# Loading token tile 2 in two partition halves on two queues, and turning it behind three K-blocks of v(0)

## The chip, the core and the metric

The kernel runs on one core of a Trainium2 chip. Its engines are TensorE (PE for matmuls, PEld for the loading of their weights), VectorE (DVE), ScalarE (ACT), GpSimd (POOL) and SyncE (SP, which here only issues DMAs). The metric is the device time of one execution in microseconds (us); a profiled execution has a span, from the first to the last instruction of the program, and a time of its own that is a little longer than the span.

## What is computed

The input x holds 2048 tokens of width 512 in bf16. Two branches read the same layer-normalised x, and both are added to x:

```python
xn = layernorm(x)                        # no scale, no shift
# branch A: linear attention, 32 heads of width 16
q, k, v = split(xn @ wqkv)               # wqkv is 512 x 1536
phi(z) = [softmax(z @ w_phi), softmax(-z @ w_phi)]
o = phi(q) @ (phi(k)^T v) / (phi(q) @ sum(phi(k)) + 1e-6)
# branch B: a gated product, inner width 1792
h = (xn @ w_gate) * (xn @ w_up)
out = x + o @ wo + h @ w_down
```

## The kernel before

**Tiles.** The tokens are cut into 16 tiles of 128 (tile t holds every fourth token of a block of 512). A tile of x is 128 partitions by 512 elements, 128 KB. Every product needs the normalised tile turned, so that the 512 features lie on partitions: four blocks of 128 features (the K-blocks 0 to 3), called `xnT` with the halves `("xnT", t, 0)` (K-blocks 0 and 1) and `("xnT", t, 1)` (K-blocks 2 and 3).

**The first four tiles.** Tiles 0 to 3 take a path of their own at the start of the program, because nothing else is there for TensorE to do. For such a tile the mean is taken in two halves of the row, one by ACT and one by DVE (`ln_mean_split`: the ACT instruction at L228 and the DVE instruction at L427, each followed by a short read of its accumulator). The mean is then subtracted by DVE (`ln_center_split` at L434 in two instructions for tiles 0 and 1, `ln_center_whole` at L439 in one for tiles 2 and 3). The scale by the standard deviation is deferred to later places. TensorE turns the centred tile by four 128x128 transposes (`x_transpose`, two calls of two transposes, L474), and ACT copies K-blocks 0 and 1 from PSUM to `xnT` (L228) while DVE copies K-blocks 2 and 3 (L483); for tile 1, DVE copies both halves.

**v of tiles 0 and 1.** `v_matmul(t, b, qs)` is a product of tile t with K-blocks of the v weights into PSUM bank b: one 128x512 matmul for each K-block (L247). The weights of K-block q are loaded by `load_v(eng, q)`, 128 KB each. K-blocks 0 and 1 of both tiles come first, then K-block 3 of both, then the four transposes of tile 2, then K-block 2 of both. Then come the four matmuls of v(2), the four transposes of tile 3, and the gate and up products, whose weights are `load_gu(..., 0, ...)`.

**What sets the order.** The loads of the start are a list written out by hand, each on SP's queue or on ACT's:

```python
    load_x(0, 1)
    load_x(1, 1, ACT)
    load_v(SP, 0)
    load_v(ACT, 1)
    load_x(2, 1)
    load_v(ACT, 3)
    load_v(SP, 2)
    load_x(3, 1)
    load_gu(SP, 0, (1,))
```

The compute steps of the start are pinned (`sc.pin`): every engine takes them in the order in which they are written. Later steps are placed by a planner (`_order`) with modelled costs. Each engine runs its own list strictly in order, and a step waits for the semaphores of the steps that it reads from. A step that reads data of two DMAs waits for two semaphores. The PE list, from the first real work on: transposes of tiles 0 and 1, K-blocks 0 and 1 of v(0) and v(1), and so on as above. In front of it stand eight `warm` matmuls on constants (L1001), the last of which waits for tile 0 of x.

Of the kernel before, what the change touches and what calls it, by code (L numbers as in the profile page):

```python
# [13 lines left out]
PE, ACT, DVE, POOL, SP = "PE", "ACT", "DVE", "POOL", "SP"  # L14
# [95 lines left out]
def bass_parallel_sum__linear_kernel_hedgehog__glu_gated_bilinear__prompt_kernel(  # L110
    nc: bass.Bass,
    A_x: bass.AP,
    A_wqkv: bass.AP,
    A_w_phi: bass.AP,
    A_wo: bass.AP,
    B_x: bass.AP,
    B_w_gate: bass.AP,
    B_w_up: bass.AP,
    B_w_down: bass.AP,
    out: bass.AP,  # L120
):
    with ExitStack() as es:
        _build(nc, es, A_x, A_wqkv, A_w_phi, A_wo, B_w_gate, B_w_up, B_w_down, out)


def _build(nc, es, A_x, A_wqkv, A_w_phi, A_wo, B_w_gate, B_w_up, B_w_down, out):
# [77 lines left out]
    def sb(name, lo, n):  # L204
        off = layout[name] + lo
        return arena[:, off:off + n]
# [4 lines left out]
    def sbf(name, lo, n):  # L211
        off = layout[name] + 2 * lo
        return arena[:, off:off + 2 * n].bitcast(F32)

    def bank(b, lo=0, n=512):
        return psum[:, b * 512 + lo:b * 512 + lo + n]

    def bank16(b, lo, n):
        return psum16[:, b * 1024 + lo:b * 1024 + lo + n]

    sc = _Sched()

    def act(out_ap, in_ap, reads, writes, func=ACTF.Copy, scale=1.0, bias=None, accum=None):
        kw = {} if bias is None else {"bias": bias}
        if accum is not None:
            kw["accum_out"] = accum
        n = out_ap.free_size()
        return sc.step(ACT, lambda e: e.activation(out=out_ap, in_=in_ap, func=func, scale=scale, **kw),  # L228
                       reads, writes, 130.0 + 0.833 * n)

    def dve(fn, reads, writes, n, rate=1.04):
        return sc.step(DVE, fn, reads, writes, 140.0 + rate * n)
# [7 lines left out]
    def mm(out_ap, pairs, reads, b, start=True, stop=True, skip=False, also=()):  # L240
        npair = len(pairs)

        def fn(e):
            ins = None
            for i, (l, r) in enumerate(pairs):
                kw = {"skip_group_check": True} if skip else {}
                ins = e.matmul(out_ap, lhsT=l, rhs=r, start=start and i == 0, stop=stop and i == npair - 1, **kw)  # L247
            return ins
        return sc.step(PE, fn, reads, [("ps", b), *also], npair * pe_cost(out_ap.free_size()))

    x_flat = A_x.flatten_outer_dims()
# [6 lines left out]
    def x_tile(t):  # L258
        return sb("x", t * 512, 512)

    def xnT(q, lo, n):
        return sb("xnT", q * S_TOK + lo, n)


    def rows(ap, t0, n):
        g, r = divmod(t0, 4)
        return ap[g * 512:(g + 1) * 512, :].rearrange("(p r) d -> p r d", r=4)[:, r:r + n, :]

    def load_x(t0, n, eng=SP):
        o = sb("x", t0 * 512, n * 512).rearrange("p (t d) -> p t d", t=n)  # L270
        i = rows(x_flat, t0, n)
        sc.dma(eng, lambda e: e.dma_start(o, i), [], [("x", t) for t in range(t0, t0 + n)], n * 131072)

    def xr_tile(t):
        return sb("xr", (t % 4) * 512, 512)

# [29 lines left out]
    def load_v(eng, q):  # L306
        load_w(eng, wv_v[:, q, :], A_wqkv[q * 128:(q + 1) * 128, 1024:1536], ("wv", q), 131072)
# [16 lines left out]
    load_x(1, 1, ACT)  # L324
    load_v(SP, 0)
    load_v(ACT, 1)
    load_x(2, 1)
    load_v(ACT, 3)
    load_v(SP, 2)
    load_x(3, 1)  # L330
# [63 lines left out]
    def xn_tile(t):  # L394
        return sb("xn", (t % 4) * 512, 512)

    mu = sbf("mu", 0, ND)
# [24 lines left out]
    mua = sbf("mua", 0, ND)  # L422

    def ln_mean_split(t):
        act(xn_tile(t)[:, 256:], x_tile(t)[:, 256:], [("x", t)], [("mu", t)], scale=1.0 / 512.0,
            accum=mu[:, t:t + 1])
        dve(lambda e: e.tensor_scalar(out=xn_tile(t)[:, :256], in0=x_tile(t)[:, :256], scalar1=1.0 / 512.0,  # L427
                                      scalar2=0.0, op0=ALU.mult, op1=ALU.add, accum_out=mua[:, t:t + 1]),
            [("x", t)], [("mua", t)], 256)

    def ln_center_split(t):
        for h in range(2):
# [5 lines left out]
    def ln_center_whole(t):  # L438
        dve(lambda e: e.tensor_scalar(out=xn_tile(t), in0=x_tile(t), scalar1=mua[:, t:t + 1],  # L439
                                      scalar2=mu[:, t:t + 1], op0=ALU.subtract, op1=ALU.subtract),  # L440
            [("x", t), ("mua", t), ("mu", t)], [("xn", t, 0)], 512, 0.27)
# [24 lines left out]
    def x_transpose(t, b, h, eng=ACT):  # L466
        n = NQ // 2
        qs = slice(h * n, (h + 1) * n)

        def fn(e):  # L470
            ins = None
            for i in range(n):
                q = h * n + i
                ins = e.transpose(bank16(b, i * 128, 128), xn_tile(t)[:, q * 128:(q + 1) * 128], ident)  # L474
            return ins
        sc.step(PE, fn, [("xn", t, h if t < 2 else 0), "ident"], [("ps", b)], n * 60.0)
        o = sb("xnT", 0, NQ * S_TOK).rearrange("p (q s) -> p q s", q=NQ)[:, qs, t * 128:(t + 1) * 128]
        i = bank16(b, 0, n * 128).rearrange("p (q s) -> p q s", q=n)
        w = [("xnT", t, h)]
        if eng == ACT:  # L480
            act(o, i, [("ps", b)], w)
        else:
            dve(lambda e: e.tensor_copy(out=o, in_=i), [("ps", b)], w, n * 128)  # L483
# [45 lines left out]
    def v_matmul(t, b, qs=((0, 1), (2, 3)), start=True, stop=True):  # L529
        for n, part in enumerate(qs):  # L530
            mm(bank(b), [(xnT(q, t * 128, 128), wv_v[:, q, :]) for q in part],
               ([("xnT", t, part[0] // 2)] if t < ND else [("xnT", t)]) + [("wv", q) for q in part], b,
               start=start and n == 0, stop=stop and n == len(qs) - 1)
# [398 lines left out]
    def out_pair(p, fill):  # L932
# [14 lines left out]
        def sum_w(k):  # L947
            return tw[k], two[k], [("tw", k), ("two", k)]
        x0 = xr_tile(t0)
        product((p, 1), BA, raw_a(t0, 0), raw_w(0, 0), True)  # L950
        seed(BB, BA)
# [6 lines left out]
        s7_2 = s7[:, None, :].to_broadcast([128, 2, 256])  # L958
        pool(lambda e: e.tensor_tensor(out=xs.rearrange("p (b c) -> p b c", b=2), in0=s7_2,  # L959
                                       in1=xr_tile(t1).rearrange("p (b c) -> p b c", b=2), op=ALU.add),  # L960
             ["s7", ("xr", t1 % 4)], ["xs"], 512)
        product((p, 3), BB, sum_a(2), sum_w(2))
# [34 lines left out]
    def warm(n, w=512, after=()):  # L997
        def fn(e):
            ins = None
            for _ in range(n):  # L1000
                ins = e.matmul(bank(7, 0, w), lhsT=nc.const_aps.tensor(1.0, (128, 128), BF16),  # L1001
                               rhs=nc.const_aps.tensor(1.0, (128, w), BF16), start=True, stop=True)
            return ins
        sc.step(PE, fn, after, [("ps", 7)], n * w * 0.8)

    warm(7)
    warm(1, 512, [("x", 0)])
    sc.pin = True
    ln_mean_split(0)
    ln_mean_split(1)  # L1010
    ln_center_split(0)
    ln_center_split(1)
    x_transpose(0, 2, 0)
    x_transpose(0, 3, 1)
    warm(1, 128)
    x_transpose(1, 4, 0, DVE)
    ln_mean_split(2)
    x_transpose(1, 5, 1, DVE)
    warm(1, 128)
    ln_center_whole(2)  # L1020
    for t in range(2):
        v_matmul(t, t, ((0, 1),), stop=False)
    for t in range(2):
        v_matmul(t, t, ((3,),), start=False, stop=False)
    x_transpose(2, 6, 0)
    x_transpose(2, 4, 1, DVE)
    for t in range(2):
        v_matmul(t, t, ((2,),), start=False)
    ln_mean_split(3)
    ln_center_whole(3)  # L1030
    (g0a, u0a, g0b, u0b), gate0 = up_unit(*ups.pop(0), pairs, 2)
# [363 lines left out]
```

## Time and profile before

| | |
|---|---|
| runs | 213.91, 214.06, 214.47, 214.66, 214.69 us (median 214.47) |
| profiled execution | 214.02 us, span 212.3 us |
| PE busy | 208.5 us, 98% of the span, 1476 matmuls |
| PEld busy | 125.2 us, 59% |
| DVE busy | 167.3 us, 79% |
| ACT busy | 143.7 us, 68% |
| POOL busy | 110.0 us, 52% |
| granted TensorE clock | 1.0 |
| DMA | 22.29 MB, mean 105 GB/s |

The busy time of an engine is the union of its instructions. Matmuls are pipelined: each appears in the trace with its own latency, so that consecutive ones overlap, and a short wait between two of them can lie under the tail of the first and not show as idle time. The distance from one start to the next tells more. A DMA appears twice: as the instruction on SP or ACT that issues it, and as its landing, some microseconds later, which is when its semaphore lets the readers go.

### The profile page before, as it was taken

How to read it: one execution, taken by the hardware profiler on the slowest of the kernel's cores; microseconds unless marked ns; L12 is line 12 of the kernel's file. 1: busy time of each engine (PE TensorE's matmuls, PEld its weight loads, DVE VectorE, ACT ScalarE, POOL GpSimd, SP SyncE). 2: the span in 40 equal slices, each digit the busy share in tenths (PEclk: the TensorE clock that was granted, in tenths of full speed). 3: DMA queues.
4: the chain of work that ended last, by engine and by line, in shares of the span. 5: the costliest groups of instructions: out<-in, count | busy, mean ns of one | idle time of the engine just before them, and what ended most of it. 6: DMA issues, size and time to landing. Idle time of an engine off the chain costs nothing.

```text
span 212.3 us, 4049 instructions
## 1 busy us (share of the span) xinstructions
PE 208.5 (98%) x1476; PEld 125.2 (59%) x1476; DVE 167.3 (79%) x281; ACT 143.7 (68%) x350; POOL 110.0 (52%) x137
## 2 busy tenths in 40 slices
PE   7999999999999999999999999999999999999995
PEld 2574444444544444444444444556888898899884
DVE  3777999986995647578699988986888898898622
ACT  4489899975789999988778977564534444432220
POOL 4031554540320366999995872004558659558540
PEclk9999999999999999999999999999999999999999
DMA  5999890799100140322720330414265746637411
GB/s 175 301 295 376 127 217 0 73 362 186 25 3 0 8 90 3 53 58 43 78 56 18 76 75 0 130 43 51 50 77 125 176 76 150 144 83 175 123 49 49
DMA packets 49251, 22.29 MB, mean 105 GB/s; under 512 B 38096, under 2 KB 47696, under 8 KB 49232
## 3 DMA queue, kind: packets, MB, share of 16 engines
q1 hardware_dynamic: 48272, 21.39, 46.0%
q10 hardware_dynamic: 960, 0.66, 1.0%
q8 instruction: 11, 0.18, 0.4%
q14 instruction: 8, 0.07, 0.2%
HBM read 11.03 MB, written 2.10 MB: 62 GB/s over the span
## 4 chain that ended last, share of the span: by engine, by line
PE 97%; DMA 1%; DVE 1%; issue 0%
PE ps L247 91%; PE ps L553 2%; PE ps L611 2%; DMA arena<-in_A_x_dram 1%; PE ps L381 1%; PE ps L474 1%; DVE arena L427 0%; DVE arena L924 0%; DVE arena L434 0%; PE ps L1001 0%
## 5 line engine op out<-in xcount | busy, mean ns | idle before, releaser
L247 PE MATMUL ps<-arena 128*128 128x512 bf16 (+2 forms) x1160 | 199.8, 330 | 0.0
L247 PEld LDWEIGHTS ps<-arena 128*128 128x128 bf16 (+1 forms) x1160 | 110.8, 98 | 73.1 <-ACT arena L228 0.9
L228 ACT ACTIVATE arena<-ps 128x512 bf16<-128x512 f32 (+3 forms) x117 | 58.6, 539 | 12.7 <-PE ps L247 8.0
L228 ACT ACTIVATE arena<-arena 128x32 f32<-128x32 f32 (+9 forms) x131 | 52.9, 423 | 11.0 <-DVE arena L506 6.8
L894 DVE TENSOR_TENSOR arena<-ps,arena 128x512 f16<-128x512 f32 (+1 forms) x56 | 38.3, 684 | 11.7 <-PE ps L247 6.1
L516 POOL TENSOR_TENSOR arena<-arena 128x1024 bf16<-128x1024 bf16 x16 | 31.8, 1995 | 26.4 <-ACT arena L228 26.4
L506 DVE TENSOR_REDUCE arena<-arena 128x64 f32<-128x1024 bf16 x32 | 38.2, 1211 | 7.8 <-ACT arena L228 7.6
L228 ACT ACTIVATE arena<-ps,arena 128x512 bf16<-128x512 f32 (+1 forms) x55 | 35.9, 671 | 10.9 <-PE ps L247 10.4
L855 POOL TENSOR_TENSOR arena<-arena 128x256 f16<-128x256 f16 x32 | 23.9, 756 | 14.1 <-DMA arena<-arena 12.9
L833 DVE TENSOR_TENSOR arena<-arena 128x896 f16<-128x896 f16 x32 | 26.0, 812 | 3.4 <-PE ps L247 3.4
L228 ACT ACTIVATE ps<-ps 128x256 f32<-128x256 f32 x24 | 8.8, 368 | 29.0 <-PE ps L247 27.0
L924 DVE SCALAR_TENSOR_TENSOR arena<-ps,arena 128x256 bf16<-128x256 f32 (+1 forms) x24 | 13.2, 566 | 8.8 <-PE ps L247 8.7
L773 POOL TENSOR_TENSOR arena<-arena 128x512 f16<-128x512 bf16 x14 | 16.3, 1174 | 5.7 <-DVE arena L894 5.2
L959 POOL TENSOR_TENSOR arena<-arena 128x512 f32<-128x512 f32 x8 | 9.5, 1191 | 17.0 <-ACT arena L228 17.0
L522 POOL TENSOR_TENSOR arena<-arena 128x512 bf16<-128x512 bf16 x16 | 16.9, 1059 | 0.8
L621 DVE TENSOR_TENSOR arena<-ps,arena 128x512 f16<-128x512 f32 x16 | 11.0, 686 | 1.3 <-ACT arena L228 0.5
L405 DVE BATCH_NORM_STATS2 arena<-arena 128x6 f32<-128x512 bf16 x16 | 10.4, 670 | 0.5 <-DMA arena<-in_A_x_dram 0.5
L520 POOL TENSOR_TENSOR arena<-arena 128x32 f32<-128x32 f32 x16 | 5.2, 326 | 10.6 <-ACT arena L228 6.0
L452 POOL TENSOR_SCALAR arena<-arena 128x1 f32<-128x1 f32 x12 | 3.2, 282 | 12.3 <-ACT arena L228 12.3
L668 DVE BATCH_NORM_STATS2 arena<-arena 128x6 f32<-128x512 bf16 x14 | 8.9, 681 | 0.0
L553 PEld LDWEIGHTS ps<-arena 128*128 128x128 bf16 x128 | 6.1, 97 | 3.5
L454 DVE TENSOR_SCALAR arena<-arena 128x512 bf16<-128x512 bf16 x12 | 5.4, 486 | 2.2 <-DMA arena<-arena 2.0
(54 smaller groups left out, 72.7 us busy)
## 6 DMA issues: line engine op xcount, KB each, us to landing
arena<-in_A_x_dram SPq DMA_DIRECT2D x8, 256.0 KB, 3.4
out_dram<-arena SPq DMA_DIRECT2D x15, 128.0 KB, 2.0
arena<-in_B_w_down_dram SPq DMA_DIRECT2D x1, 1792.0 KB, 9.6
arena<-in_A_x_dram SPq DMA_DIRECT2D x3, 512.0 KB, 4.6
arena<-arena SPq DMA_TRANSPOSE x44, 3.1
arena<-in_B_w_gate_dram SPq DMA_DIRECT2D x1, 640.0 KB, 8.7
arena<-in_B_w_up_dram SPq DMA_DIRECT2D x1, 640.0 KB, 9.9
arena<-in_B_w_gate_dram SPq DMA_DIRECT2D x1, 512.0 KB, 5.1
```

What stands on the lines that cost most here:

```text
L228: return sc.step(ACT, lambda e: e.activation(out=out_ap, in_=in_ap, func=func, scale=scale, **kw), reads, writes, 130.0 + 0.833 * n)
L247: ins = e.matmul(out_ap, lhsT=l, rhs=r, start=start and i == 0, stop=stop and i == npair - 1, **kw)
L405: dve(lambda e: e.bn_stats(stats_v[:, t, 0:6], x_tile(t)), [("x", t)], [("st", t)], 512)
L506: dve(lambda e: e.tensor_reduce(out=sm, in_=e_v, axis=AX.X, op=ALU.add), [(name, s, 0), (name, s, 1)], [("sums", sr)], 1024)
L516: pool(lambda e: e.tensor_tensor(out=e_w, in0=e_w, in1=r_w, op=ALU.mult), [(name, s, 0), (name, s, 1), ("rs", n)], [(name, s, 0), (name, s ...
L522: pool(lambda e: e.tensor_tensor(out=e_v[:, :, 1, :], in0=e_v[:, :, 1, :], in1=rat[:, :, None].to_broadcast([128, H, 16]), op=ALU.mult), [ ...
L621: dve(lambda e: e.tensor_tensor(out=o_tile(t).rearrange("p (b h f) -> p b h f", b=2, f=16), in0=nd[:, :, :, 0:16], in1=w_v[:, r].unsqueeze ...
L773: pool(lambda e, ft=ft: e.tensor_tensor(out=hH_v[:, ft, 0:512], in0=hT_v[:, ft, 0:512], in1=r2w, op=ALU.mult), [("hT", ft, 0), "r2w", ("x" ...
L833: dve(lambda e, k=k, i0=i0, i1=i1, op=op: e.tensor_tensor(out=s_block(p, k), in0=i0, in1=i1, op=op), ks + more, [s_key(p, k)] + over.get(k ...
L855: pool(lambda e, k=k, i0=i0, i1=i1, op=op: e.tensor_tensor(out=so_block(p, k), in0=i0, in1=i1, op=op), ks + [("so", p, m) for m in more], ...
L894: dve(lambda e: e.tensor_tensor(out=h_v[:, ft, sg * 512:(sg + 1) * 512], in0=bank(bu), in1=g, op=ALU.mult), [("ps", bu), ("g", s)] + ([("j ...
L924: dve(lambda e: e.scalar_tensor_tensor(out=o, in0=src, scalar=inv, in1=resid, op0=ALU.mult, op1=ALU.add), keys + [rkey, "inv"], [("ostg", ...
```

## The change

The load of tile 2 is split into partitions 0 to 63 on SP's queue and partitions 64 to 127 on ACT's queue. Both halves stand where the whole tile stood on SP's queue; on ACT's queue the half stands ahead of the weights of K-block 3. The two mean instructions of tile 2 wait for both halves. DVE centres tile 2 before it copies K-blocks 2 and 3 of tile 1. On PE the transposes of tile 2 come behind three K-blocks of v(0) (0, 1 and 3) and two of v(1); K-block 3 of v(1) goes behind K-block 2 of v(0). No matmul, transpose or copy is added or taken out. One DMA is added, and all the bytes are the same. On PE, ACT, DVE, POOL and SP the lists are otherwise identical to those of before, all the way to the end.

```diff
+    def load_x_half(t, h, eng):
+        p = slice(h * 64, h * 64 + 64)
+        o, i = x_tile(t)[p, :], rows(x_flat, t, 1)[p, 0, :]
+        sc.dma(eng, lambda e: e.dma_start(o, i), [], [("x", t) if h else ("x", t, 0)], 65536)
...
     load_x(1, 1, ACT)
     load_v(SP, 0)
     load_v(ACT, 1)
-    load_x(2, 1)
+    load_x_half(2, 0, SP)
+    load_x_half(2, 1, ACT)
     load_v(ACT, 3)
     load_v(SP, 2)
     load_x(3, 1)
...
     def ln_mean_split(t):
-        act(xn_tile(t)[:, 256:], x_tile(t)[:, 256:], [("x", t)], [("mu", t)], scale=1.0 / 512.0,
+        xs_k = [("x", t)] + [("x", t, 0)] * (t == 2)
+        act(xn_tile(t)[:, 256:], x_tile(t)[:, 256:], xs_k, [("mu", t)], scale=1.0 / 512.0,
             accum=mu[:, t:t + 1])
         dve(lambda e: e.tensor_scalar(out=xn_tile(t)[:, :256], in0=x_tile(t)[:, :256], scalar1=1.0 / 512.0,
                                       scalar2=0.0, op0=ALU.mult, op1=ALU.add, accum_out=mua[:, t:t + 1]),
-            [("x", t)], [("mua", t)], 256)
+            xs_k, [("mua", t)], 256)
...
     x_transpose(1, 4, 0, DVE)
     ln_mean_split(2)
+    ln_center_whole(2)
     x_transpose(1, 5, 1, DVE)
     warm(1, 128)
-    ln_center_whole(2)
     for t in range(2):
         v_matmul(t, t, ((0, 1),), stop=False)
-    for t in range(2):
-        v_matmul(t, t, ((3,),), start=False, stop=False)
+    v_matmul(0, 0, ((3,),), start=False, stop=False)
     x_transpose(2, 6, 0)
     x_transpose(2, 4, 1, DVE)
-    for t in range(2):
-        v_matmul(t, t, ((2,),), start=False)
+    v_matmul(0, 0, ((2,),), start=False)
+    v_matmul(1, 1, ((3,), (2,)), start=False)
     ln_mean_split(3)
     ln_center_whole(3)
```

## The prediction

> **What bounds the kernel now.** I read the page first: which engine is busy, and what the chain that ended last consists of.
>
> ```profile
> PE 208.5 (98%) x1476; PEld 125.2 (59%) x1476; DVE 167.3 (79%) x281; ACT 143.7 (68%) x350; POOL 110.0 (52%) x137
> ...
> PE 97%; DMA 1%; DVE 1%; issue 0%
> ```
>
> TensorE is the bound, and its work stays the same: no matmul is added or taken out. So the change can only pay where PE waits. The part it touches is the start, so next I read PE's timeline from 5.6 to 9.0 us (start, length, engine, line, count), and by how much PE's weight loads were held up (in brackets).
>
> ```profile
> 5.66 1.46 PE L247 MATMUL ps<-arena 128*128 128x512 bf16 x6
> 6.95 0.39 PE L474 MATMUL ps<-arena 128*128 128x128 bf16 x4
> 7.17 1.56 PE L247 MATMUL ps<-arena 128*128 128x512 bf16 x6
> 8.62 0.40 PE L474 MATMUL ps<-arena 128*128 128x128 bf16 x4
> 8.85 0.38 PE L247 MATMUL ps<-arena 128*128 128x256 bf16 x2
> ...
> 6.89 0.27 PEld L474 LDWEIGHTS ps<-arena 128*128 128x128 bf16 x4 [0.23 <-DVE arena L439]
> ...
> 7.70 0.55 PEld L247 LDWEIGHTS ps<-arena 128*128 128x128 bf16 x4 [0.42 <-ACT arena L228]
> 8.61 0.23 PEld L474 LDWEIGHTS ps<-arena 128*128 128x128 bf16 x4 [0.37 <-DVE arena L439]
> ```
>
> The starts count, as lengths overlap. Six 128x512 matmuls from 5.66 to 6.95 are 1.29 us, 0.216 each, without a gap (they are K-blocks 0 and 1 of v(0) and v(1), then K-block 3 of both). Four transposes of tile 2 take 0.22. The next six should be over at 7.17 + 1.29 = 8.46, but the transposes of tile 3 begin at 8.62: **PE loses 0.16 us here**. Some 0.10 of it lies before v(2), which could begin at 7.17 + 2 x 0.216 = 7.60 and waits for ACT's copy of tile 2 until 7.70; the other 0.06 before the transposes of tile 3, which wait for DVE's centring. From 8.85 on the same count of starts shows no further wait of PE over 0.03 us up to its last matmul. So 0.16 us of 214 is all that a better order of the start can bring; the bracketed idle times of PEld are larger only because weights are loaded ahead.
>
> Then I read who holds tile 2, on DVE and ACT:
>
> ```profile
> 5.67 0.42 ACT L228 ACTIVATE arena<-arena 128x256 bf16<-128x256 bf16 x1
> 5.98 0.20 ACT L228 ACTIVATION_READ_ACCUMULATOR arena<-arena 128x1 f32 x1
> 7.26 0.38 ACT L228 ACTIVATE arena<-ps 128x256 bf16<-128x256 bf16 x1 [1.08 <-PE ps L474]
> ...
> 5.90 0.41 DVE L427 TENSOR_SCALAR_CACHE_REDUCE arena<-arena 128x256 bf16<-128x256 bf16 x1
> 6.23 0.08 DVE L427 DVE_READ_ACCUMULATOR arena<-arena 128x1 f32 x1
> 6.23 0.29 DVE L483 COPY arena<-ps 128x256 bf16<-128x256 bf16 x1
> 6.43 0.41 DVE L439 TENSOR_SCALAR arena<-arena 128x512 bf16<-128x512 bf16 x1
> ```
>
> The mean of tile 2 begins at 5.67 on ACT and 5.90 on DVE, each directly behind the copies of tiles 0 and 1. Tile 2 itself was issued at 1.70 and landed 3.7 us later (the DMA view of that moment), at 5.40. So its landing isn't what the mean waits for: there are 0.27 us to spare.
>
> **The load in two halves: nothing.** Each half is issued third on its queue, where tile 2 stood on SP (landed 5.40) and the weights of K-block 3 on ACT (1.71 + 3.9 = 5.61). Both whole transfers in these places landed ahead of 5.67, so halves should as well; by half the bytes, some 0.2 us ahead of 5.40. An earlier landing brings nothing, as ACT comes to the mean only after its copies. A later one than 5.67 would move the centring one for one; I take 0. The second semaphore on each mean instruction is waited for while ACT and DVE still run the copies before it.
>
> The Trainium skill, "DMA: Bandwidth & Descriptors", section "Rules for kernel authors", speaks against this edit: it says of two transfers to disjoint partition halves "Don't bother — they serialize", since both use the same 16 DMA engines. By that rule the tile would land no earlier than 5.40, and the sum would be the same, as nothing here is priced on an earlier landing.
>
> **What is queued behind the added DMA.** One issue on ACT's queue costs 0.42 to 0.45 us. It pushes the issue of K-block 3's weights from 1.71 to 2.17 and of the first gate weights from 2.23 to 2.68, ended 3.13. ACT's first mean starts at 3.61, so 0.48 us of cover remain; without cover the mean of tile 0, at the head of PE's chain, would move by the 0.45. SP issues as often as before. The rows for what landed when (issue, and time to landing in us):
>
> ```profile
> arena<-in_A_wqkv_dram SPq DMA_DIRECT2D x1, 128.0 KB, 3.9
> arena<-in_A_x_dram SPq DMA_DIRECT2D x1, 128.0 KB, 4.7
> arena<-in_B_w_gate_dram ACTq DMA_DIRECT2D x1, 256.0 KB, 5.1
> ```
>
> These were issued at 2.17, 2.64 and 2.23 and landed at 6.07, 7.34 and 7.33. K-block 3 now has the place of the first row on the other queue: it lands between 5.61 (as before) and 7.34 (one place further back). I take 6.07, whose issue time and bytes ahead are nearest. PE needs it at 6.52: no cost, 0.45 to spare. The gate weights are needed at 8.85 and would have to come 1.5 us later to matter; up weights (issued 3.12 + 5.1 = 8.22) keep their issue.
>
> **DVE's order: tile 2 centred earlier.** The centring goes ahead of the copy at 6.23. Its inputs: ACT's accumulator is read out by 5.98 + 0.20 = 6.18, DVE's by 6.31. For tile 3 the centring came 0.11 after ACT's read (8.04 to 8.15); behind an own result DVE went on after 0.04 (batch statistics end 9.94, aggregate 9.98). So it starts at max(6.18 + 0.11, 6.31 + 0.04) = 6.35, at worst 6.31 + 0.11 = 6.42, against 6.43. That is 0.08 gained, 0.01 at least. It ends 0.41 later, 6.76, and PE starts 0.06 behind such an end (8.56 to 8.62): tile 2's transposes can start at **6.82** (to 6.89).
>
> **PE's order.** K-block 3 of v(1), 0.216 us, goes from before the transposes to behind them, so PE is there at 5.66 + 5 x 0.216 = 6.74 and stands 0.08 us (to 0.15). A new wait, then, and what is queued behind it is everything. On from 6.82: four transposes to 7.04, three matmuls (K-block 2 of v(0), 3 and 2 of v(1)) to 7.69. The delayed DVE copy for v(1) starts some 0.33 behind the centring, is done at about 6.97 and is needed at 7.26: hidden, 0.29 to spare. ACT's copy of tile 2 starts 0.31 behind the transposes (6.95 to 7.26), so 7.13 to 7.51, and with 0.06 on to PE is ready at 7.57, ahead of 7.69: **the 0.10 wait is gone**, but 0.08 stands before it. v(2) then runs from 7.69 to 8.55. ACT's mean of tile 3 moves up from 7.54 to 7.41 (tile 3 landed by 7.34), DVE's centring from 8.15 to 8.02, done 8.43, ready for PE at 8.49, ahead of 8.55: **the 0.06 wait is gone**.
>
> **The sum.** The transposes of tile 3 start at 8.55 in place of 8.62: **0.07 us less**, with bounds of 0 (centring at 6.42) and 0.16 (no wait left). Behind that PE is without gaps and passes it to the end. The profiled execution took 214.02 us, 1.7 over its span, and becomes 213.95; the median of the runs is 214.47, so I forecast **214.40**. That is 0.03%, where about 0.3% (0.64 us) is what a measurement of this kernel can tell from no change.
>
> **Rivals.**
>
> *Slower: PE's queue stands at K-block 3 of v(0).* Its weights are now fourth on ACT's queue, and the transposes of tile 2 and all of PE are queued behind that matmul. If they land in the last possible row's place, 7.34, it starts at about 7.39, and the tile 3 transposes at 7.39 + 0.216 + 0.22 + 3 x 0.216 + 4 x 0.216 = 9.34, against 8.62: 0.72 us slower, **215.2**. It takes a landing after 6.61 to lose anything, after 7.25 to lose 0.64. Against it: K-block 2's weights, issued at the same 2.17, landed at 6.07. Chance of over 0.3% slower, this way or another: 0.16.
>
> *Faster: the slow ones of the five runs are slow at this place.* The runs lie between 213.91 and 214.69, and only one near 214.0 was profiled. If in the others tile 2 lands after 5.67, its earlier landing brings them all to the 213.9 of the best, less the 0.07: **213.8**, 0.3% faster. For it: 0.27 us of spare time is little. Against it: a late first tile would do the same and isn't touched, and the eight warm matmuls have a pitch of 0.43 against 0.216 later, so the moment at which PE speeds up can shift a run too. Chance of over 0.3%: 0.16.
>
> "TensorE: Matmul & The Clock Gate", Part 1, of the Trainium skill says that this moment depends on a free-running window; no row here shows that.
>
> *No effect.* Centring at 6.42 or a half landing near 5.7: the new wait takes the place of the old ones, **214.47**. Chance 0.23; the forecast itself has 0.45.
>
> **How the numbers follow.** Within 0.3%: 0.45 + 0.23 = 0.68; faster 0.16, slower 0.16. The likeliest value is 214.40; by itself it would hold 214.31 to 214.47, but the runs alone spread by 0.78. The range goes to just beyond the faster case, 213.7, and close to the slower one, 215.1.
>
> **What would show it.** Right: tile 2's centring before the copy at about 6.35, PE's transposes of tile 2 at about 6.82 behind five matmuls, no gap before v(2), tile 3's transposes near 8.55. Wrong: a DMA named before K-block 3 of v(0), the mean of tile 2 later than 5.67, or a gap of PE behind 8.85 that was not there.

## The result and the profile after

The change made the kernel slower. The median over 29 runs is 214.96 us, against 214.34 us over 51 runs of the kernel before; the ratio is **1.0036, 95% interval 1.0026 to 1.0046** (it is estimated from all the runs, here and below, and isn't the quotient of the two medians). The best run went from 213.90 to 214.62. The profiled execution took 214.78 us with a span of 213.0, against 214.02 and 212.3. So some 0.6 to 0.8 us were lost, where 0.07 us less was forecast.

The profile of the changed kernel: engines, and the chain that ended last.

```profile
PE 208.4 (98%) x1476; PEld 125.3 (59%) x1476; DVE 167.5 (79%) x281; ACT 144.2 (68%) x350; POOL 110.4 (52%) x137
...
PE 95%; DMA 2%; ACTq 0%; DVE 0%; ACT 0%; issue 0%
```

PE does the same work. But its share of the chain fell from 97% to 95%, and a DMA has 2%. The first 10 us of that chain say which (start, length, what):

```profile
1.25 0.45 ACTq L297
...
1.73 0.55 ACTq L277
...
2.31 5.01 DMA arena<-in_A_wqkv_dram
7.33 0.14 issue
7.46 0.38 PE ps L247
```

Before, this chain began with the first tile of x and ran through DVE to PE:

```profile
0.79 2.80 DMA arena<-in_A_x_dram
...
3.61 0.57 DVE arena L427 x3
...
4.70 0.65 PE ps L474 x4
```

Now it begins with ACT's queue: the half of tile 2 (L277), behind it the weights of K-block 3 (L297), issued at 2.31 and landed 5.01 us later. PE's timeline has the wait in the same place:

```profile
5.67 1.03 PE L247 MATMUL ps<-arena 128*128 128x512 bf16 x4
7.46 0.38 PE L247 MATMUL ps<-arena 128*128 128x512 bf16 x1 [0.76 <-DMA arena<-in_A_wqkv_dram]
7.67 0.38 PE L481 MATMUL ps<-arena 128*128 128x128 bf16 x4
7.90 1.67 PE L247 MATMUL ps<-arena 128*128 128x512 bf16 x7
9.41 0.39 PE L481 MATMUL ps<-arena 128*128 128x128 bf16 x4
```

Four matmuls from 5.67 are through at 5.67 + 4 x 0.216 = 6.53; the fifth, K-block 3 of v(0), starts at 7.46. That is 0.92 us of waiting (0.76 of it outside the tail of the fourth). Behind it everything is without a gap, and tile 3's transposes start at 9.41 in place of 8.62. From the first gate product to the last matmul this kernel and the one before take the same 200.5 us, so the start holds the whole difference.

Why are the weights late? The issues on ACT's queue and, below, on SP's (start, length):

```profile
1.73 0.55 ACTq L277 DMA_DIRECT2D arena<-in_A_x_dram  x1
2.31 0.86 ACTq L297 DMA_DIRECT2D arena<-in_A_wqkv_dram  x1
...
3.23 0.42 ACTq L297 DMA_DIRECT2D arena<-in_B_w_gate_dram  x1
...
1.71 0.57 SPq L277 DMA_DIRECT2D arena<-in_A_x_dram  x1
2.32 0.57 SPq L297 DMA_DIRECT2D arena<-in_A_wqkv_dram  x1
2.94 0.43 SPq L272 DMA_DIRECT2D arena<-in_A_x_dram  x1
```

In the kernel before, the third to fifth loads of SP's queue were the whole tile 2, the weights of K-block 2 and tile 3; on ACT's queue the weights of K-blocks 1 and 3 (one line, x2) came ahead of the gate weights:

```profile
1.70 0.42 SPq L272 DMA_DIRECT2D arena<-in_A_x_dram  x1
2.17 0.43 SPq L292 DMA_DIRECT2D arena<-in_A_wqkv_dram  x1
2.64 0.43 SPq L272 DMA_DIRECT2D arena<-in_A_x_dram  x1
...
1.23 0.93 ACTq L292 DMA_DIRECT2D arena<-in_A_wqkv_dram  x2
2.23 0.42 ACTq L292 DMA_DIRECT2D arena<-in_B_w_gate_dram  x1
```

A half takes 0.55 or 0.57 us to issue, a whole tile took 0.42. The load *behind* a half is slow too: 0.57 on SP, 0.86 on ACT. Then the transfers run thin. The stretch from 4.0 to 5.5 us, first of the kernel before and then of this one (the last two columns are the DMA engines' busy share and GB/s):

```profile
4.00:5.50 1.50, 1.20 (x9) 0.60 (x9) 1.41 (x8) 0.89 (x6) 0.00 (x0) 1.00 0.97 307
```

```profile
4.00:5.50 1.50, 1.12 (x9) 0.41 (x8) 1.44 (x8) 1.06 (x6) 0.00 (x0) 1.00 0.66 189
```

### The profile page after: what moved, and what is told of

Read it like the earlier page. It is cut to its first block, busy times and chain, and to the rows that moved or that the text cites. A ratio compares the mean times of both kernels' runs of the same rounds, so it can differ in the third digit from the quotient of the medians.

```text
span 213.0 us, 4052 instructions
## 1 busy us (share of the span) xinstructions
PE 208.4 (98%) x1476; PEld 125.3 (59%) x1476; DVE 167.5 (79%) x281; ACT 144.2 (68%) x350; POOL 110.4 (52%) x137
## 4 chain that ended last, share of the span: by engine, by line
PE 95%; DMA 2%; ACTq 0%; DVE 0%; ACT 0%; issue 0%
PE ps L247 90%; DMA arena<-in_A_wqkv_dram 2%; PE ps L560 2%; PE ps L618 2%; PE ps L387 1%; ACTq L277 0%; DVE arena L931 0%; ACTq L297 0%; PE ps L481 0%; ACT L1201 0%
## 5 line engine op out<-in xcount | busy, mean ns | idle before, releaser
L560 PEld LDWEIGHTS ps<-arena 128*128 128x128 bf16 x128 | 6.1, 97 | 3.5
L618 PEld LDWEIGHTS ps<-arena 128*128 128x128 bf16 x128 | 6.2, 97 | 1.2
```

The source lines that it names most:

```text
L618: ins = e.matmul(bank(b0 + c // 4, (c % 4) * CW, CW), lhsT=ph[:, c, :], rhs=kvz_v[:, c, :], start=True, stop=True)
```

## The experiments

Theories after the result: **(1)** a load of 64 partitions is dear to issue and slows the issue behind it; **(2)** the place of K-block 3's weights, fourth on ACT's queue, is what matters, whatever is ahead; **(3)** one load more in flight is enough to lose the time. Against all three stood the new order of DVE and PE as a cause. Every ratio and every "over before" below is to runs of the kernel before on the same chip beside it (12 runs each, 28 to 35 of before). Three dots in a diff stand for lines left out, mostly the change of the waits that goes with a load.

**The order without the loads.** The changed kernel with the old load list:

```diff
-    load_x_half(2, 0, SP)
-    load_x_half(2, 1, ACT)
+    load_x(2, 1)
...
```

> The new order of DVE and PE alone; all loads as in the kernel before (tile 2 whole, third on SP). All three theories say the same: K-block 3's weights land at about 5.6 as before, no wait of PE before K-block 3 of v(0), the transposes of tile 3 start 0.05 to 0.15 us earlier than the 8.62 of before. Time 0.0 to 0.2 us less than before; a ratio within 0.2% of 1.

Measured: median 214.31 against 214.21, ratio 1.0002 (0.9983 to 1.0021). PE and DVE in its profile:

```profile
5.72 1.24 PE L247 MATMUL ps<-arena 128*128 128x512 bf16 x5
6.81 0.40 PE L480 MATMUL ps<-arena 128*128 128x128 bf16 x4
7.04 1.67 PE L247 MATMUL ps<-arena 128*128 128x512 bf16 x7
8.55 0.39 PE L480 MATMUL ps<-arena 128*128 128x128 bf16 x4
...
6.34 0.41 DVE L445 TENSOR_SCALAR arena<-arena 128x512 bf16<-128x512 bf16 x1
```

Five matmuls from 5.72 are through at 6.80, and the transposes start at 6.81; seven from 7.04 end at 8.55, and tile 3's start at 8.55. Both old waits of PE are gone and no new one is there. From the first v matmul to the first gate product it is 3.06 us, against 3.19 before. In the profile the order does what it was priced for; in the median 0.13 us can't be told from nothing.

**The loads without the order.** The changed kernel's loads, the old order of DVE and PE. Against the kernel before:

```diff
     load_x(1, 1, ACT)
     load_v(SP, 0)
     load_v(ACT, 1)
-    load_x(2, 1)
+    load_x_half(2, 0, SP)
+    load_x_half(2, 1, ACT)
...
```

> The two half loads alone; the order of DVE and PE as in the kernel before. Loss is in the loads: PE waits about 0.9 us before K-block 3 of v(0), the weights land at about 7.3, and the time is 0.6 to 1.0 us over before (PE's old wait of 0.10 before v(2) comes back on top of the changed kernel's). If the loss were in the order, this would be within 0.2 us of before.

Measured: median 214.96, 0.75 over before, ratio 1.0028 (1.0011 to 1.0045). K-block 3's weights land at 7.03, and PE waits 0.63 us there. The issues are the same to 0.01 us as in the changed kernel (0.57, 0.55, 0.86, 0.57).

```profile
5.67 1.03 PE L247 MATMUL ps<-arena 128*128 128x512 bf16 x4
7.17 0.59 PE L247 MATMUL ps<-arena 128*128 128x512 bf16 x2 [0.47 <-DMA arena<-in_A_wqkv_dram]
```

**The loss is in the loads.**

**Which part of the loads: the place.** Tile 2 whole, by one load, where ACT's half stood; SP has none.

```diff
-    load_x_half(2, 0, SP)
-    load_x_half(2, 1, ACT)
+    load_x(2, 1, ACT)
...
```

> The changed kernel, but tile 2 is loaded whole (128 partitions) by one DMA on ACT's queue, in the place of the ACT half, and SP has one load less. Theory 1, a DMA of 64 partitions is dear to issue and delays its queue: the weights of K-block 3, still fourth on ACT, are issued at 2.17 and land at 6.0 to 6.3, PE does not wait for them, time within 0.2 us of before. Theory 2, the place on ACT's queue: they land at 7.2 or later as in the changed kernel, 0.6 us or more over before. Theory 3, one DMA more in flight: as theory 1, since there is no added DMA here.

> A second profile of the kernel with tile 2 whole on ACT's queue, since the first profile was one of its longer executions. Theory 1: issue times of 0.42 to 0.45 us again; K-block 3's weights land between 6.2 and 7.5, one place further back than before, and PE waits 0 to 1 us, according to the landing.

Measured: median 214.46, 0.25 over before, ratio 1.0009 (0.9988 to 1.0030). Issues are at 0.42 to 0.45 again. But the landing was a miss for theory 1: in the two profiled executions, both among the long ones of this kernel (215.01 and 215.32), K-block 3's weights landed at 7.54 and 7.21. So in single executions the place can cost as much as the halves do. In the median it is a third of the 0.75, and the interval holds no change at all.

**Which part: one load more, or the form.** Halves by columns: 128 partitions, 512 bytes of each.

```diff
-        p = slice(h * 64, h * 64 + 64)
-        o, i = x_tile(t)[p, :], rows(x_flat, t, 1)[p, 0, :]
+        c = slice(h * 256, h * 256 + 256)
+        o, i = x_tile(t)[:, c], rows(x_flat, t, 1)[:, 0, c]
```

> The changed kernel, but the two halves are the columns 0 to 255 and 256 to 511 of all 128 partitions, in the same places on the same queues. Theory 1, 64 partitions are dear: issues take 0.42 to 0.45 us again, K-block 3's weights land at 6.0 to 6.4, time within 0.2 us of before. Theories 2 (place on ACT's queue) and 3 (one DMA more): they land at 7 or later, 0.5 us or more over before.

Measured: median 214.37, 0.16 over before, ratio 1.0001 (0.9986 to 1.0017); the interval lies clear of the changed kernel's. ACT's issues:

```profile
1.71 0.45 ACTq L277 DMA_DIRECT2D arena<-in_A_x_dram  x1
2.20 0.45 ACTq L297 DMA_DIRECT2D arena<-in_A_wqkv_dram  x1
```

The same number of loads, the same bytes, the same places, and 0.45 in place of 0.55 and 0.86. But in the profiled execution, one of its longest (214.60), K-block 3's weights land at 6.76, later than the 6.0 to 6.4 of theory 1, and PE waits 0.43 us for them, and later for the gate weights (landed 9.42):

```profile
6.89 0.38 PE L247 MATMUL ps<-arena 128*128 128x512 bf16 x1 [0.26 <-DMA arena<-in_A_wqkv_dram]
```

The best run is 0.28 over the best of before, where the changed kernel's was 0.72 over. So theories 2 and 3, which expected 0.5 us or more here, don't carry the loss. The added slot costs something between nothing (by the ratio) and 0.28 us (by the best run), and the form of 64 partitions the rest.

**The form, parted from its size.** Tiles 2 and 3 together in two loads of 64 partitions, 128 KB each, and no load of tile 3:

```diff
-        o, i = x_tile(t)[p, :], rows(x_flat, t, 1)[p, 0, :]
+        o = sb("x", t * 512, 1024).rearrange("p (t d) -> p t d", t=2)[p]
+        i = rows(x_flat, t, 2)[p]
...
-    load_x(3, 1)
...
```

> Tiles 2 and 3 together in two loads of 64 partitions, 2 KB for each partition, one on SP and one on ACT in the places of the halves of tile 2; the load of tile 3 is gone. So the halves carry 128 KB each, and the form (64 partitions) is parted from the small size. If the form itself is dear: issues of 0.53 to 0.57 us and a slow one behind them, K-block 3's weights landing at 7 or later, 0.5 us or more over before. If a dear issue comes from the small size: issues of 0.42 to 0.45 us. In both cases K-block 3's weights have 384 KB ahead of them on ACT's queue, so they land no earlier than 6.2.

Measured: median 215.55, 1.26 over before, ratio 1.0050 (1.0030 to 1.0070). ACT's issues:

```profile
1.73 0.55 ACTq L278 DMA_DIRECT2D arena<-in_A_x_dram  x1
2.31 0.84 ACTq L298 DMA_DIRECT2D arena<-in_A_wqkv_dram  x1
```

The form is dear to issue at 128 KB as well. The profiled execution was the fastest of the twelve (214.62; K-block 3's weights landed at 6.92 and the gate weights at 9.38), so no trace shows where the 1.26 of the median goes. **And it isn't simply "few partitions":** four quarters of 32 partitions, two on each queue.

```diff
-        p = slice(h * 64, h * 64 + 64)
+        p = slice(h * 32, h * 32 + 32)
...
-    load_x_half(2, 0, SP)
-    load_x_half(2, 1, ACT)
+    for h in range(4):
+        load_x_half(2, h, (SP, ACT)[h % 2])
...
```

> The suspected cost doubled: the changed kernel with tile 2 in four quarters of 32 partitions, two on each queue, same bytes. Theory 1 (a load of few partitions is dear to issue, and an issue slot moves few bytes): four slots of 0.5 us or more ahead of the v weights, these issued at 2.8 or later and K-block 3 landing at 7.5 to 8.5; PE waits 1.0 to 2.0 us, time 1.0 to 1.8 us over before. If only the place of K-block 3 on ACT's queue counted, and not what stands ahead of it in slots and form, the loss would stay at 0.6 to 0.8.

Measured: median 214.79, 0.50 over before, ratio 1.0013 (0.9995 to 1.0031): a miss of theory 1 as I had put it. Tile 2 lands early, at 5.41, K-block 3's weights at 6.87 cost PE nothing in the profile, and it waits 0.4 us for tile 3 (landed 8.24). The first of these is luck: PE's first v matmuls were slow in this execution (see the end), and at a pitch of 0.216 PE would have come to these weights at 5.76 + 4 x 0.216 = 6.62. ACT's issues:

```profile
1.72 0.92 ACTq L277 DMA_DIRECT2D arena<-in_A_x_dram  x2
2.67 0.45 ACTq L297 DMA_DIRECT2D arena<-in_A_wqkv_dram  x1
```

Two quarters are issued in 0.92, 0.45 each, and the load behind them in 0.45. Two cheap quarters cost ACT's queue less than one half and its aftermath: the weights' issue ends at 3.12, against 3.17 in the changed kernel. That is nearly the same moment, and in time the quarters can't be told from the halves: what is shown to be special about 64 partitions is the price of the issue, not a larger loss than two more slots bring.

**The form on one queue.** Both halves of tile 2 on SP:

```diff
-    load_x_half(2, 1, ACT)
+    load_x_half(2, 1, SP)
```

> The changed kernel, but both partition halves of tile 2 are issued on SP's queue, one behind the other; ACT's queue is as in the kernel before. Theory 1 (a load of 64 partitions is dear to issue and slows the issue behind it, whichever queue has it): halves take 0.55 to 0.6 us to issue, the load behind them 0.55 or more; K-block 3's weights on ACT land at 5.6 to 6.0 and PE does not wait there; K-block 2's weights on SP are issued at 2.8 or later, land at 7.0 or later and PE waits 0.3 us or more behind the transposes of tile 2. Time 0.3 to 0.9 us over before. Rival (the two halves disturb each other because both queues issue them at the same moment): issues are back at 0.42 to 0.45, time within 0.3 us of before.

Measured: median 214.72, 0.50 over before, ratio 1.0031 (1.0015 to 1.0047). SP's issues are 0.57 and 0.59 for the halves and 0.59 for the load behind them, so it takes no second queue. K-block 3's weights land at 5.95 and nothing waits there. PE waits earlier than expected: before the transposes of tile 2, 0.42 us, as the second half lands at 6.30. ACT's issues beside them stayed at 0.42 to 0.46.

**The form where it disturbs least.** The new order, tile 2 whole, and tile 3 in two halves on SP:

```diff
-    load_x(3, 1)
+    load_x_half(3, 0, SP)
+    load_x_half(3, 1, SP)
...
```

> The disputed cost by itself: the new order of DVE and PE, tile 2 whole and third on SP as before, ACT's queue as before, and tile 3 in two halves of 64 partitions on SP, fourth and fifth behind it. Theory 1: two issues of 0.55 to 0.6 us in place of one of 0.43, and 0.55 for the up weights behind them; K-block 3's weights land at 5.6 to 5.9 and nothing waits at K-block 3; tile 3 lands at 7.3 to 8.0, PE waits 0 to 0.4 us before the transposes of tile 3 or the up weights. Time 0 to 0.4 us over before.

Measured: median 214.55, 0.27 over before, ratio 1.0011 (0.9989 to 1.0033). Issues of 0.56, 0.59 and, behind them, 0.59: the same price again. The profiled execution was the longest of its twelve (215.74), and in it tile 2, whole and third on SP as in the kernel before, landed at 7.29 in place of 5.40, and K-block 3's weights at 7.50, where 5.6 to 5.9 was expected. More on that below.

**Moving the wait away from K-block 3.** Two experiments. First, ACT's half behind the weights:

```diff
     load_x_half(2, 0, SP)
-    load_x_half(2, 1, ACT)
     load_v(ACT, 3)
+    load_x_half(2, 1, ACT)
```

> The changed kernel, but ACT's half of tile 2 stands behind the weights of K-block 3. These are issued third on ACT again, at 1.73, and land at 5.6 to 6.0, so the wait of 0.9 us before K-block 3 of v(0) is gone. Theory 1: the half takes 0.55 us to issue and the gate weights behind it about 0.85; the half lands at 6.0 to 6.6, PE waits 0.3 to 0.9 us before the transposes of tile 2, and the gate weights land after 9. Time 0.3 to 0.8 us over before. If the place ahead of K-block 3 were all of the loss, time would be within 0.2 us of before.

Measured: median 215.00, 0.78 over before, ratio 1.0032 (1.0015 to 1.0049). The weights land at 5.18, but the half only at 6.93 (expected 6.0 to 6.6): PE waits 1.46 us before the transposes of tile 2 in place of K-block 3, where 0.3 to 0.9 was expected. Second, the K-blocks exchanged on PE:

```diff
-    v_matmul(0, 0, ((3,),), start=False, stop=False)
+    v_matmul(0, 0, ((2,),), start=False, stop=False)
...
-    v_matmul(0, 0, ((2,),), start=False)
-    v_matmul(1, 1, ((3,), (2,)), start=False)
+    v_matmul(1, 1, ((2,),), start=False, stop=False)
+    v_matmul(0, 0, ((3,),), start=False)
+    v_matmul(1, 1, ((3,),), start=False)
```

> The changed kernel with K-blocks 2 and 3 exchanged on PE for v(0) and v(1): the weights that land first (6.55 in the changed kernel's profile, against 7.33) are used first. If the late weights of K-block 3 are all of the loss: the wait shrinks from 0.92 to about 0.35 us, time 0.4 to 0.5 us less than the changed kernel. If the gate weights (landing at 9.60, just as PE came to them at 9.64) are the next in line: the wait moves to the gate products, PE reaches them no earlier than 9.6, and the time is that of the changed kernel within 0.15 us, 0.5 to 0.8 over before.

Measured: median 214.94, 0.72 over before, ratio 1.0035 (1.0017 to 1.0053), the changed kernel's. Its PE timeline:

```profile
7.06 0.38 PE L247 MATMUL ps<-arena 128*128 128x512 bf16 x1 [0.37 <-DMA arena<-in_A_wqkv_dram]
...
9.01 0.39 PE L481 MATMUL ps<-arena 128*128 128x128 bf16 x4
9.81 0.39 PE L247 MATMUL ps<-arena 128*128 128x256 bf16 x2 [0.42 <-DMA arena<-in_B_w_gate_dram]
```

The wait is split in two. PE waits for K-block 2 until 7.06, and the transposes of tile 3 come at 9.01, 0.4 earlier than in the changed kernel. But the gate weights land at 9.77, and the gate products start at 9.81. All that was saved is given back there: **the gate weights are next in line**. In the profile of the loads alone it is the same: they land at 9.68 and the gate products start at 9.72. Another order of the v matmuls doesn't help when the gate weights are late too.

## Why the prediction was wrong

**Bound and place: right.** PE is the bound, and only the start could move. The 200.5 us behind the first gate product came out the same.

**DVE's and PE's order: right.** With the old loads, the step forecast 6.35 for the centring, 6.82 for tile 2's transposes and 8.55 for tile 3's; measured were 6.34, 6.81 and 8.55. That the clock times agree so well is partly luck: PE started 0.06 us later, and the "new wait" of 0.08 before tile 2's transposes came out at 0.01, since DVE's mean instruction began 0.08 us earlier (5.82 against 5.90). Counted from PE's start the gain is 0.13 and not 0.07, within the bounds given. In the changed kernel the centring comes at 6.23, and waits no longer matter there.

**The load in two halves, "nothing", and what is queued behind the added DMA: wrong, and this is the step that failed.** The landing of tile 2 itself was right in the changed kernel's profile, 5.25 and 5.47, ahead of 5.67; but with the same loads ACT's half landed at 5.91 and 5.92 in the profiles of the loads alone and of K-block 2 first, so that term isn't safe either. The step that failed is the term "K-block 3 lands at 6.07: no cost, 0.45 to spare"; it measured 7.33 and cost 0.92 us. The mis-sized terms in it and beside it:
- "One issue on ACT's queue costs 0.42 to 0.45 us" was read from loads of 128 partitions. A half took 0.55, and the load behind it 0.86. The weights' issue began at 2.31 in place of 2.17 and ended at 3.17, where 2.17 + 0.45 = 2.62 was assumed. So 0.55 of the 1.26 us by which the landing was off lies at the issue.
- K-block 3's landing was taken as 6.07, by the row with the nearest issue time and bytes ahead. It came at 7.33, the far end that I had bounded at 7.34. The row was of the other queue, with loads of 128 partitions alone ahead of it, and from 4.0 to 5.5 us the transfers had fallen from 307 to 189 GB/s. From the end of the issue to the landing it took 4.16 us, where 3.45 was assumed; it was 3.86 and 4.42 in the two other profiles with these loads and 4.11 with column halves, so this part is not the form's alone.
- "The gate weights would have to come 1.5 us later to matter": they came 2.27 us later (9.60 against 7.33), hidden only because PE was late as well.
- "0.48 us of cover remain" before ACT's first mean: none did. ACT's last issue ended at 3.65 in place of 3.13, and the mean of tile 0 began at 3.70 on ACT, 0.12 us after DVE's (3.58). It cost nothing here, as PE waited for K-block 3's weights in any case.

**The rivals.** The slower one is what happened: its matmul was put at 7.39 and started at 7.46, tile 3's transposes were put at 9.34 and started at 9.41. Its place and mechanism were right, its chance, 0.16, too small: it was held small by one row of the kernel before, although the shape of the load ahead had changed. That the landing met its bound to 0.01 us is luck: with the same loads it was 7.03 and 7.58 in other profiles, and the bound came from a place further back in the queue, not from the price of an issue. The faster rival did not come about: no kernel with a split tile 2 has a median or a best run below those of the kernel before. Its premise, that long executions are long because tile 2 lands late, is not refuted: in the one of 215.74 us with tile 2 whole in its old place, it landed at 7.29, but so did K-block 3's weights, at 7.50.

**The rule on partition halves.** The Trainium skill, "DMA: Bandwidth & Descriptors", section "Rules for kernel authors", says not to bother with two transfers to disjoint partition halves. The advice held. Its reason, that both use the same DMA engines, would have left the time unchanged; what the runs show is a price at the issue (0.55 and 0.86 against 0.42 and 0.45) that it does not speak of.

**What stays open.** Why 64 partitions are dear to issue and 32 or 128 are not, and why the load behind pays as well, no run here shows. Nor is it settled why the transfers thin out: from 4.0 to 5.5 us the single profiles give 189, 135 and 135 GB/s with halves on both queues ahead of the weights, 175 with quarters, 205 with halves of two tiles, 214 with column halves, 227 and 251 with tile 2 whole on ACT, 273 with the order alone, but 301 with both halves on SP. So thin transfers are not the mark of 64 partitions. How much of the loss comes by the price of the issue and how much by the transfers behind it is not shown: the quarters, with cheap issues, lost 0.50 us in the median as well.

## What to carry to other kernels

Where a start lives on the issue of its loads, count issue slots and look at the shape of each: a load with half of the bytes takes a slot all the same, and here one of 64 partitions took more than one. What is queued behind an added load is priced from its own issue and from the shape of what stands ahead of it, not from a row with other loads ahead, and when a bound reaches 1.3 us beyond the value taken, one such row is too little to call it unlikely. A step that gains (here 0.13 us by the order, in one profile) is best run without the step that only seems free.

## What the runs showed of the hardware that was not expected

- A load of 64 partitions took 0.53 to 0.59 us to issue in all seven kernels that had one, with 1 KB or 2 KB for each partition, on SP and on ACT; loads of x and of the v weights with 32 or 128 partitions and no half ahead of them took 0.39 to 0.46. The load behind it took 0.56 to 0.59, and 0.84 to 0.86 on ACT when both queues had issued a half at the same time. In one kernel (ACT's half behind the weights) the load after that on SP took 0.56 as well.
- The same load in the same place lands at very different times: tile 2, whole and third on SP with the same loads ahead on both queues, at 5.40, 5.70 and 7.29 in the profiles of three kernels. One profile can't bound a landing.
- The moment at which PE goes from a pitch of 0.43 us to 0.216 for a 128x512 matmul moves from one execution to another. In the profile with tile 2 in quarters the first v matmuls are still slow (the first two pitches are 0.43 and 0.40 us); the five below take 7.23 - 5.76 = 1.47 us, and the five with the order alone 1.09. The granted clock didn't tell the two apart: it stood at 1.0 in both.

```profile
5.76 1.64 PE L247 MATMUL ps<-arena 128*128 128x512 bf16 x5
7.23 0.39 PE L481 MATMUL ps<-arena 128*128 128x128 bf16 x4
```
